# Where tile 5 is transposed, and how the first half of chunk 0 is blocked, in a layernorm, local attention and GLU kernel

## The chip, the cores and the metric

The kernel runs on one core of one Trainium2 chip. The core has five engines that this text names: TensorE (PE in the profile, PEld for its weight loads), VectorE (DVE), ScalarE (ACT), GpSimd (POOL) and SyncE (SP), which issues all of this kernel's DMAs. The metric is the device time of one execution in microseconds (us). The kernel before takes 228.16 us, the median of three runs (227.9 to 228.41).

## What is computed

One layernorm of x (2048 tokens of 512) feeds two branches, whose product is added to x: a dilated local attention (32 heads of 16, 8 positions 2 apart) and a gated linear unit with 1792 inner columns. All inputs and the output are bfloat16.

```python
def reference(A_x, A_wqkv, A_wo, B_x, B_w_gate, B_w_up, B_w_down):
    x = A_x                                        # 1 x 2048 x 512
    xn = layernorm(x)
    # attention: H = 32, Dh = 16, W = 8, dil = 2
    q, k, v = heads(xn @ A_wqkv)
    idx = pos[:, None] - arange(W) * dil           # masked where idx < 0
    logits = einsum("bhsd,bhswd->bhsw", q, k[idx]) * Dh ** -0.5
    s = einsum("bhsw,bhswd->bhsd", softmax(logits), v[idx]) @ A_wo
    # gated linear unit
    h = gelu(xn @ B_w_gate) * (xn @ B_w_up)
    return x + s * silu(h @ B_w_down)
```

## The kernel before

The 2048 tokens are 16 tiles of 128, in four chunks of four tiles (512 tokens). Chunk 0 has the tiles 0 to 3, chunk 1 the tiles 4 to 7. For each chunk j TensorE needs xnT[j], the normalized tokens transposed, so that the 512 features lie on the partitions in four blocks dk.

Order of the program (written out by hand; nothing reorders it, and `at` and `run` only hang pieces of work onto a place in the loops):

- *Loads*, all issued by SP in order: tiles 0 and 1 of x, three row blocks of wqkv, tiles 2 and 3, the last block of wqkv, tiles 4 to 7, then halves of the gate and up weights with the rest of x. A DMA waits for the DMA eight before it, since there are eight completion semaphores that go round.
- *Chunk 0, first half of the tokens (tiles 0 and 1, 256 tokens)*. Six groups of PSUM, `pairs`, hold two output blocks of 128 columns of wqkv each (v in two PSUM tiles of the pool mm, q and k in the tile quad), zeroed first by a matmul with `zero` (L542). `block(dk, ns, i0, n)` (L547 to L557) adds contraction block dk of wqkv to the groups ns for n tokens from i0. Contraction block 0 runs apart for tile 0 (128 tokens) and for tile 1. A tile's way to xnT is: VectorE's statistics (L188, L191), ScalarE's square root (L192), VectorE's reciprocal and `normalize` (xn, L213), four transposes on TensorE into PSUM (L221), and a copy into xnT on ScalarE (L232) or VectorE (L234). Tiles 0 and 1 go in two steps, feature block 0 first and then the other three, through the PSUM tiles tra and trb. The transposes of tiles 2 and 3 stand among the matmuls of block 3 (L593 to L597).
- *Chunk 0, second half (tiles 2 and 3)*. Six groups of two output blocks (L605 to L612); the first group runs in slices of 128 tokens, so that its first half needs tile 2 only. `copy_out` brings q and k to SBUF and v to vst, and SP stores vst to vT in DRAM (L292).
- *GLU of chunk 0*, 14 steps of eight matmuls (g_ps, u_ps; L263). Tiles 4 and 5 are transposed on TensorE ahead of steps 0 and 1. Onto step 0 are also hung, in SP's order: two DMA transposes of tile 6 (`transpose_by_dma`, L255, one DMA for each feature block), the four loads of v from vT with a shift for each position (`load_v`, L308, into v_arr), six DMA transposes (rest of tile 6, tile 7), and the late weights wd and wo (L117, L120). VectorE makes the products of q and k (pk, L334) and h (L449); from step 11 on it makes the products of attention weights and v (pv, L406, eight in all).
- *Chunk 1's projection* (L298, 48 matmuls of 512 tokens, reading all four tiles of xnT[1]), then the down projection of chunk 0 (y_ps, L457, reading wd and h), the denominators and sums (den_ps L372, o_ps L420, reading the eight pv), the logits of chunk 1 (L_ps L352, reading chunk 1's pk), and the output of chunk 0. The other chunks follow in the same way, all their tiles transposed by DMA.

Of the kernel before, what the change touches and what calls it, by code (L numbers as in the profile page):

```python
# [10 lines left out]
BF16 = mybir.dt.bfloat16  # L11
F32 = mybir.dt.float32

P = 128
# [14 lines left out]
def kernel(  # L29
# [13 lines left out]
    nc = tc.nc  # L43
    B, S, D = A_x.shape
    DF = B_w_gate.shape[1]
    NT, NC, NF, NJ = S // P, D // P, DF // P, S // TQ
    TPQ = TQ // P
# [5 lines left out]
    def pool(name, bufs, **kw):  # L53
        return ctx.enter_context(tc.tile_pool(name=name, bufs=bufs, **kw))
# [19 lines left out]
    mm = pool("mm", 4, space=bass.MemoryType.PSUM)  # L74
# [4 lines left out]
    wqkv_sb = wts.tile([P, NC, 3 * D], BF16, name="wqkv_sb")  # L79
# [7 lines left out]
    def load_x(t, n=1):  # L87
        nc.sync.dma_start(
            out=x_sb[:, t : t + n, :],
            in_=x2d[t * P : (t + n) * P, :].rearrange("(t p) d -> p t d", p=P),  # L90
        )
# [7 lines left out]
    def load_wqkv(k):  # L99
        nc.sync.dma_start(out=wqkv_sb[:, k, :], in_=A_wqkv[k * P : (k + 1) * P, :])  # L100

    load_x(0)
    load_x(1)
    load_wqkv(0)
    load_wqkv(1)
    load_wqkv(2)
    load_x(2)
    load_x(3)
    load_wqkv(3)
    load_x(TPQ, TPQ)  # L110
    for i, (lo, hi) in enumerate(((0, DF // 2), (DF // 2, DF))):
        load_w(wg_sb, B_w_gate, lo, hi)
# [19 lines left out]
    ident = const.tile([P, P], BF16, name="ident")  # L132
# [38 lines left out]
    xnT = {}  # L171
# [15 lines left out]
    def first_stats(t):  # L187
        nc.vector.bn_stats(out=stats[:, t, :], in_=x_sb[:, t, :])  # L188

    def first_moments(t):  # L190
        nc.vector.bn_aggr(out=mv[:, t, :], in_=stats[:, t, :])  # L191
        nc.scalar.activation(  # L192
            out=std[:, t, :], in_=mv[:, t, 1:2], func=AF.Sqrt, bias=epsc[:], scale=1.0
        )

    def first_rstd(t):
        nc.vector.reciprocal(out=rstd[:, t, :], in_=std[:, t, :])
# [9 lines left out]
    xns = {}  # L207

    def normalize(t, cs=range(NC)):
        if 0 in cs:  # L210
            xns[t] = xnp.tile([P, D], BF16, name="xn")
        cols = slice(cs[0] * P, (cs[-1] + 1) * P)
        nc.vector.tensor_scalar(  # L213
            out=xns[t][:, cols], in0=x_sb[:, t, cols],
            scalar1=mv[:, t, 0:1], scalar2=rstd[:, t, :],
            op0=ALU.subtract, op1=ALU.mult,
        )

    def to_psum(t, cs, tr):
        for n, c in enumerate(cs):  # L220
            nc.tensor.transpose(  # L221
                tr[:, n * P : (n + 1) * P], xns[t][:, c * P : (c + 1) * P], ident[:]
            )

    def from_psum(t, cs, tr, copy=None):
        j, i = divmod(t, TPQ)
        if j not in xnT:
            xnT[j] = xtp.tile([P, NC, TQ], BF16, name="xnT")
        dst = xnT[j][:, cs[0] : cs[-1] + 1, i * P : (i + 1) * P]
        src = tr.rearrange("p (c n) -> p c n", c=len(cs))  # L230
        if copy is None:
            nc.scalar.activation(out=dst, in_=src, func=AF.Copy)  # L232
        else:
            copy(out=dst, in_=src)  # L234

    def transpose(t, copy=None):
        tr = mm.tile([P, NC * P], BF16, name="tr", tag="mm")
        to_psum(t, range(NC), tr[:])
        from_psum(t, range(NC), tr[:], copy)

    def warm_up(n, cols):

        ps = mm.tile([P, TQ], F32, name="warm_ps", tag="mm")
        for _ in range(n):
            nc.tensor.matmul(  # L245
                ps[:, 0:cols], lhsT=nc.const_aps.tensor(1.0, [P, P], BF16),
                rhs=nc.const_aps.tensor(1.0, [P, cols], BF16), start=True, stop=True,
            )
# [12 lines left out]
    def project(ps, w, lo, j, i0=0, n=TQ):  # L261
        for dk in range(NC):
            nc.tensor.matmul(  # L263
                ps,
                lhsT=w[:, dk, lo : lo + P],
                rhs=xnT[j][:, dk, i0 : i0 + n],
                start=(dk == 0),
                stop=(dk == NC - 1),
            )
# [3 lines left out]
    def copy_out(j, fo, ps, i0=0, n=TQ, m=1, copy=None):  # L273

        which, c = divmod(fo, NC)
        if which == 0:
            if "q" not in st[j]:
                st[j]["q"] = qp.tile([P, NC, TQ], BF16, name="q_sb")
            dst = st[j]["q"][:, c : c + m, i0 : i0 + n]
        elif which == 1:  # L280
            dst = k_sb[j][:, c : c + m, PAD + i0 : PAD + i0 + n]
        else:
            if c // 2 not in st[j]["vst"]:
                st[j]["vst"][c // 2] = vsp.tile([P, 2, TQ], BF16, name="vst")
            dst = st[j]["vst"][c // 2][:, c % 2 : c % 2 + m, i0 : i0 + n]
        if copy is None:
            nc.scalar.activation(out=dst, in_=ps, func=AF.Copy)  # L287
        else:
            copy(out=dst, in_=ps)
        if which == 2 and (c + m) % 2 == 0 and i0 + n == TQ:  # L290
            r, lo = slice((c // 2) * 2 * P, (c // 2 + 1) * 2 * P), PAD + j * TQ
            nc.sync.dma_start(  # L292
                out=vT[r, lo : lo + TQ].rearrange("(c p) n -> p c n", p=P),
                in_=st[j]["vst"][c // 2][:],
            )
# [193 lines left out]
    def at(key, fn, *args):  # L489
        side.setdefault(key, []).append((fn, args))  # L490
# [4 lines left out]

    for i in range(TPQ):
        at(("down", 0, 1), moments, 2 * TPQ + i)
        if i < 2:
            at(("glu", 0, i), transpose, TPQ + i)
        at(("down", 0, 2), normalize, 2 * TPQ + i)  # L500
        at(("glu", 1, 0) if i else ("down", 0, 3), transpose_by_dma, 2 * TPQ + i)
        at(("glu", 1, 10 + i), moments, 3 * TPQ + i)
        at(("qkv", 2, i), normalize, 3 * TPQ + i)
        at(("glu", 2, 0) if i else ("down", 1, 3), transpose_by_dma, 3 * TPQ + i)
# [31 lines left out]
    HQ = TPQ // 2 * P  # L536
    warm_up(6, TQ // 2)
    quad = att.tile([P, NC, 2, HQ], F32, name="qk_ps", tag="quad")
    pairs = [(8 + 2 * i, mm.tile([P, 2, HQ], F32, name="v_ps", tag="mm")[:]) for i in range(2)]
    pairs += [(2 * i, quad[:, i]) for i in range(4)]  # L540
    for _, ps in pairs:
        nc.tensor.matmul(  # L542
            ps, lhsT=zero[:], rhs=nc.const_aps.tensor(1.0, [P, 2, HQ], BF16),
            start=True, stop=False,
        )
    warm_up(4, P)
    def block(dk, ns, i0=0, n=HQ):  # L547
        for b in ns:
            fo, ps = pairs[b]
            for i in range(2):  # L550
                nc.tensor.matmul(  # L551
                    ps[:, i, i0 : i0 + n],
                    lhsT=wqkv_sb[:, dk, (fo + i) * P : (fo + i + 1) * P],
                    rhs=xnT[0][:, dk, i0 : i0 + n],
                    start=False,
                    stop=(dk == NC - 1 and i == 1),
                )  # L557


    one, rest = [0], range(1, NC)  # L560
    tra = mm.tile([P, 2, P], BF16, name="tra", tag="mm")
    trb = mm.tile([P, 2, (NC - 1) * P], BF16, name="trb", tag="mm")
    first_stats(0)
    first_moments(0)
    first_stats(1)
    first_rstd(0)
    first_moments(1)
    normalize(0, one)
    to_psum(0, one, tra[:, 0])
    from_psum(0, one, tra[:, 0])  # L570
    normalize(0, rest)
    to_psum(0, rest, trb[:, 0])
    from_psum(0, rest, trb[:, 0])
    first_rstd(1)
    normalize(1, one)
    normalize(1, rest)
    block(0, range(2), 0, P)
    to_psum(1, one, tra[:, 1])
    from_psum(1, one, tra[:, 1], nc.vector.tensor_copy)
    block(0, range(2, 6), 0, P)  # L580
    to_psum(1, rest, trb[:, 1])
    from_psum(1, rest, trb[:, 1], nc.vector.tensor_copy)
    block(0, range(6), P, P)
    for t in (2, 3):
        first_stats(t)
        first_moments(t)
    nc.scalar.preload_act_table(AF.Gelu_apprx_tanh)
    for t in (2, 3):
        first_rstd(t)
        normalize(t)  # L590
    block(1, range(6))
    block(2, range(6))
    block(3, range(3))  # L593
    transpose(2, nc.vector.tensor_copy)
    block(3, range(3, 5))
    transpose(3, nc.vector.tensor_copy)
    block(3, range(5, 6))  # L597
    for fo, ps in pairs:
        copy_out(0, fo, ps, 0, HQ, 2, nc.vector.tensor_copy if fo >= 8 else None)
    for t in range(TPQ, 2 * TPQ, 2):  # L600
# [3 lines left out]
    sum_constants()  # L604
    for n, fo in enumerate((0, 2, 4, 6, 8, 10)):  # L605
        ps = mm.tile([P, 2, HQ], F32, name="qkv_ps", tag="mm")

        w = HQ if n else P
        for i0 in range(0, HQ, w):
            for i in range(2):  # L610
                project(ps[:, i, i0 : i0 + w], wqkv_sb, (fo + i) * P, 0, HQ + i0, w)
        copy_out(0, fo, ps[:], HQ, HQ, 2)  # L612
    at(("glu", 0, 0), transpose_by_dma, TPQ + 2, (0, 1))
    at(("glu", 0, 0), load_v, 0)
    at(("glu", 0, 0), transpose_by_dma, TPQ + 2, (2, 3))
    at(("glu", 0, 0), transpose_by_dma, TPQ + 3)
    at(("glu", 0, 0), load_late_weights)
    for j in range(NJ):
# [57 lines left out]
```

## Time and profile before

| | |
|---|---|
| median of three runs | 228.16 us |
| profiled execution | 228.41 us, of it 226.7 us span |
| PE busy | 222.4 us (98% of the span), 1342 matmuls |
| DVE busy | 152.2 us (67%) |
| ACT busy | 132.3 us (58%) |
| TensorE clock granted | full in all 40 slices of the span |

The span is what the profiler shows of the engines; the 1.7 us beside it lie around them. "Busy" is an average over stages with different limits, so a stage's own timeline decides what a change in it is worth. The busy shares in 40 slices of 5.67 us (tenths; GB/s is what the DMA engines moved) show how the stages differ: the transfers are full in the first four slices, pause in the fifth, and are busy again up to the eighth:

```profile
PE   8999999999999999999999999999999999999993
...
DVE  5588961999995489969803859925934448971434
...
DMA  6999399942049911100219941100218940001011
GB/s 191 361 397 385 102 211 162 309 121 95 6 99 198 196 48 30 21 1 0 93 34 205 191 112 23 26 6 0 92 25 167 198 113 0 0 3 30 1 39 54
```

In a timeline a row gives start and length in us, engine, line, operation, output and inputs, and in brackets how long the engine stood idle before and what ended that. A row can merge several instructions (x4), and a matmul's row is longer than its share of a stream, because matmuls overlap; the chain in order of time gives each its share of the time.

### The profile page before, as it was taken

How to read it: one execution, taken by the hardware profiler on the slowest of the kernel's cores; microseconds unless marked ns; L12 is line 12 of the kernel's file. 1: busy time of each engine (PE TensorE's matmuls, PEld its weight loads, DVE VectorE, ACT ScalarE, POOL GpSimd, SP SyncE). 2: the span in 40 equal slices, each digit the busy share in tenths (PEclk: the TensorE clock that was granted, in tenths of full speed). 3: DMA queues.
4: the chain of work that ended last, by engine and by line, in shares of the span. 5: the costliest groups of instructions: out<-in, count | busy, mean ns of one | idle time of the engine just before them, and what ended most of it. 6: DMA issues, size and time to landing. Idle time of an engine off the chain costs nothing.

```text
span 226.7 us, 3637 instructions
## 1 busy us (share of the span) xinstructions
PE 222.4 (98%) x1342; PEld 107.9 (48%) x1342; DVE 152.2 (67%) x281; ACT 132.3 (58%) x209; POOL 21.4 (9%) x67
## 2 busy tenths in 40 slices
PE   8999999999999999999999999999999999999993
PEld 4995444444444444444444444444444444444453
DVE  5588961999995489969803859925934448971434
ACT  4388679767631767676752466676763356756210
POOL 1025961000040000320000000000000000000000
PEclk9999999999999999999999999999999999999999
DMA  6999399942049911100219941100218940001011
GB/s 191 361 397 385 102 211 162 309 121 95 6 99 198 196 48 30 21 1 0 93 34 205 191 112 23 26 6 0 92 25 167 198 113 0 0 3 30 1 39 54
DMA packets 30130, 24.64 MB, mean 109 GB/s; under 512 B 10784, under 2 KB 29600, under 8 KB 30112
## 3 DMA queue, kind: packets, MB, share of 16 engines
q1 hardware_dynamic: 30112, 24.41, 45.1%
q8 instruction: 10, 0.16, 0.3%
q14 instruction: 8, 0.07, 0.1%
HBM read 18.74 MB, written 4.34 MB: 102 GB/s over the span
## 4 chain that ended last, share of the span: by engine, by line
PE 98%; DVE 0%; issue 0%; DVEq 0%
PE y_ps L457 21%; PE g_ps L263 21%; PE u_ps L263 21%; PE qkv_ps L263 16%; PE s_ps L473 6%; PE L_ps L352 3%; PE o_ps L420 3%; PE qk_ps L551 2%; PE v_ps L551 1%; PE warm_ps L245 1%; PE qk_ps L542 1%; PE den_ps L372 0%; PE tr L221 0%; PE v_ps L542 0%; PE trb L221 0%; DVE m L481 0%
## 5 line engine op out<-in xcount | busy, mean ns | idle before, releaser
L263 PE MATMUL g_ps<-xnT,wg_sb 128*128 128x512 bf16 x224 | 57.5, 379 | 0.0
L263 PE MATMUL u_ps<-xnT,wu_sb 128*128 128x512 bf16 x224 | 57.5, 379 | 0.0
L457 PE MATMUL y_ps<-wd_sb,h 128*128 128x512 bf16 (+1 forms) x238 | 49.9, 367 | 0.0
L447 ACT ACTIVATE u<-u_ps 128x512 bf16<-128x512 f32 x56 | 33.5, 598 | 16.9 <-PE u_ps L263 16.9
L445 ACT ACTIVATE ge<-g_ps 128x512 bf16<-128x512 f32 x56 | 33.5, 598 | 16.4 <-PE g_ps L263 16.3
L449 DVE TENSOR_TENSOR h<-ge,u 128x512 bf16<-128x512 bf16 x56 | 23.8, 425 | 28.5 <-ACT u L447 26.9
L334 DVE TENSOR_TENSOR pk<-q_sb,k_sb 128x1024 bf16<-128x1024 bf16 (+1 forms) x56 | 39.0, 760 | 4.6 <-ACT k_sb L287 4.6
L406 DVE TENSOR_TENSOR pv<-E,v_arr 128x1024 bf16<-128x1024 bf16 (+1 forms) x48 | 39.7, 862 | 0.3 <-DMA v_arr<-vT 0.3
L263 PE MATMUL qkv_ps<-xnT,wqkv_sb 128*128 128x512 bf16 (+2 forms) x200 | 37.0, 345 | 0.0
L457 PEld LDWEIGHTS <-h 128*128 128x128 bf16 x238 | 23.0, 98 | 25.9 <-issue 1.3
L263 PEld LDWEIGHTS <-wu_sb 128*128 128x128 bf16 x224 | 21.9, 98 | 26.4
L263 PEld LDWEIGHTS <-wg_sb 128*128 128x128 bf16 x224 | 21.7, 98 | 26.3 <-issue 0.8
L465 ACT ACTIVATE sl<-y_ps 128x512 bf16<-128x512 f32 (+1 forms) x17 | 9.7, 572 | 32.6 <-PE y_ps L457 32.6
L263 PEld LDWEIGHTS <-wqkv_sb 128*128 128x128 bf16 x200 | 18.9, 98 | 17.5
L481 DVE TENSOR_TENSOR m<-s_ps,sl 128x512 bf16<-128x512 f32 (+1 forms) x17 | 11.1, 655 | 18.9 <-PE s_ps L473 18.9
L432 DVE TENSOR_TENSOR oT<-o_ps,rb 128x1024 bf16<-128x1024 f32 x8 | 9.4, 1218 | 11.9 <-DMA rb<-rs_d 11.9
L205 POOL TENSOR_TENSOR rstd<-rstd,mhalf 128x1 f32<-128x1 f32 x12 | 8.1, 671 | 71.5 <-DVE rstd L202 71.5
L473 PE MATMUL s_ps<-wo_sb,oT 128*128 128x512 bf16 (+1 forms) x68 | 14.8, 366 | 0.0
L287 ACT ACTIVATE vst<-qkv_ps 128x512 bf16<-128x512 f32 x14 | 8.4, 597 | 3.7 <-PE qkv_ps L263 3.7
L287 ACT ACTIVATE k_sb<-qkv_ps 128x512 bf16<-128x512 f32 x14 | 8.4, 601 | 3.2 <-PE qkv_ps L263 3.2
L473 PEld LDWEIGHTS <-oT 128*128 128x128 bf16 x68 | 6.7, 98 | 7.2
L287 ACT ACTIVATE q_sb<-qkv_ps 128x512 bf16<-128x512 f32 x14 | 8.3, 603 | 3.0 <-PE qkv_ps L263 3.0
(64 smaller groups left out, 130.7 us busy)
## 6 DMA issues: line engine op xcount, KB each, us to landing
v_arr<-vT SPq DMA_DIRECT2D x16, 520.0 KB, 8.6
vT<-vst SPq DMA_DIRECT2D x8, 256.0 KB, 2.2
out_dram<-o_t SPq DMA_DIRECT2D x15, 128.0 KB, 3.2
wg_sb<-in_B_w_gate_dram SPq DMA_DIRECT2D x2, 896.0 KB, 10.0
wu_sb<-in_B_w_up_dram SPq DMA_DIRECT2D x2, 896.0 KB, 11.6
wd_sb<-in_B_w_down_dram SPq DMA_DIRECT2D x1, 1792.0 KB, 9.4
wqkv_sb<-in_A_wqkv_dram SPq DMA_DIRECT2D x4, 384.0 KB, 4.8
x_sb<-in_A_x_dram SPq DMA_DIRECT2D x3, 512.0 KB, 11.3
```

Source lines behind the costliest of these rows:

```text
L263: nc.tensor.matmul(ps, lhsT=w[:, dk, lo : lo + P], rhs=xnT[j][:, dk, i0 : i0 + n], start=(dk == 0), stop=(dk == NC - 1),)
L287: nc.scalar.activation(out=dst, in_=ps, func=AF.Copy)
L334: nc.vector.tensor_tensor(out=st[j]["pk"][w][:, c0 : c0 + n, :], in0=st[j]["q"][:, c0 : c0 + n, :], in1=k_sb[j][:, c0 : c0 + n, off : off ...
L406: nc.vector.tensor_tensor(out=pv[:, d : d + n, :], in0=st[j]["E"][:, wh, :].unsqueeze(1).to_broadcast([P, n, TQ]), in1=st[j]["va"][:, 4 * ...
L432: nc.vector.tensor_tensor(out=oT[:, g : g + 2, :], in0=st[j]["o"][:, g : g + 2, :], in1=st[j]["rb"][:].unsqueeze(1).to_broadcast([P, 2, TQ ...
L445: nc.scalar.activation(out=ge[:], in_=g_ps[:], func=AF.Gelu_apprx_tanh)
L447: nc.scalar.activation(out=u[:], in_=u_ps[:], func=AF.Copy)
L449: nc.vector.tensor_tensor(out=h[:], in0=ge[:], in1=u[:], op=ALU.mult)
L457: nc.tensor.matmul(y[:], lhsT=st[j][fc][:, tt * P : (tt + 1) * P], rhs=wd_sb[:, fc, cols], start=(fc == 0), stop=(fc == NF - 1),)
L465: nc.scalar.activation(out=sl[:], in_=y[:], func=AF.Silu)
L473: nc.tensor.matmul(s[:], lhsT=st[j]["oT"][:, g, tt * P : (tt + 1) * P], rhs=wo_sb[:, g, cols], start=(g == 0), stop=(g == NC - 1),)
L481: nc.vector.tensor_tensor(out=m[:], in0=s[:], in1=sl[:], op=ALU.mult)
```

## The change

The diff does four things.

1. In chunk 0's first half all contraction blocks run over 256 tokens in one loop, block 0 too. Tile 0 is normalized in one operation and transposed into one PSUM tile, from which feature block 0 and then the others are copied; two matmuls of `warm_up` follow. Tile 1 is normalized, transposed and copied in two steps as before, now from one PSUM tile.
2. Tile 2 is transposed at the end of block 2 (before: after three groups of block 3), tile 3 after three groups of block 3 (before: after five).
3. The first group of chunk 0's second half runs over 256 tokens at once, not in slices of 128.
4. Tile 4 is still transposed on TensorE ahead of step 0 of the GLU. Tile 5 is transposed by four DMAs on SP. In SP's queue now five transposes (tile 5, and feature block 0 of tile 6) stand ahead of the four loads of v, and seven (the rest of tile 6, tile 7) behind them; before it was two and six.

The loads at the start are written as loops, in the same order. The helper functions `to_psum` and `from_psum` take the PSUM tile from a table by tile number.

```diff
     def to_psum(t, cs=range(NC)):
+        if 0 in cs:
+            trs[t] = mm.tile([P, NC * P], BF16, name="tr", tag="mm")
+        for c in cs:
             nc.tensor.transpose(
+                trs[t][:, c * P : (c + 1) * P], xns[t][:, c * P : (c + 1) * P], ident[:]
+            )
...
     for i in range(TPQ):
         at(("down", 0, 1), moments, 2 * TPQ + i)
-        if i < 2:
-            at(("glu", 0, i), transpose, TPQ + i)
...
-    normalize(0, one)
-    to_psum(0, one, tra[:, 0])
-    from_psum(0, one, tra[:, 0])
-    normalize(0, rest)
-    to_psum(0, rest, trb[:, 0])
-    from_psum(0, rest, trb[:, 0])
+    normalize(0)
+    to_psum(0)
+    from_psum(0, [0])
+    from_psum(0, rest)
+    warm_up(2, P)
     first_rstd(1)
-    normalize(1, one)
+    normalize(1, [0])
     normalize(1, rest)
-    block(0, range(2), 0, P)
-    to_psum(1, one, tra[:, 1])
-    from_psum(1, one, tra[:, 1], nc.vector.tensor_copy)
-    block(0, range(2, 6), 0, P)
-    to_psum(1, rest, trb[:, 1])
-    from_psum(1, rest, trb[:, 1], nc.vector.tensor_copy)
-    block(0, range(6), P, P)
+    to_psum(1, [0])
+    from_psum(1, [0], nc.vector.tensor_copy)
+    to_psum(1, rest)
+    from_psum(1, rest, nc.vector.tensor_copy)
...
-    block(1, range(6))
-    block(2, range(6))
-    block(3, range(3))
-    transpose(2, nc.vector.tensor_copy)
-    block(3, range(3, 5))
-    transpose(3, nc.vector.tensor_copy)
-    block(3, range(5, 6))
+    for dk in range(NC):
+        for n, (fo, ps) in enumerate(pairs):
+            for i in range(2):
+                nc.tensor.matmul(
+                    ps[:, i, :],
+                    lhsT=wqkv_sb[:, dk, (fo + i) * P : (fo + i + 1) * P],
+                    rhs=xnT[0][:, dk, 0:HQ],
...
+            if (dk, n) in ((2, 5), (3, 2)):
+                transpose(dk, copy=nc.vector.tensor_copy)
...
-        w = HQ if n else P
-        for i0 in range(0, HQ, w):
-            for i in range(2):
-                project(ps[:, i, i0 : i0 + w], wqkv_sb, (fo + i) * P, 0, HQ + i0, w)
+        for i in range(2):
+            project(ps[:, i, :], wqkv_sb, (fo + i) * P, 0, HQ, HQ)
         copy_out(0, fo, ps[:], HQ, HQ, 2)
-    at(("glu", 0, 0), transpose_by_dma, TPQ + 2, (0, 1))
+    at(("glu", 0, 0), transpose, TPQ)
+    at(("glu", 0, 0), transpose_by_dma, TPQ + 1)
+    at(("glu", 0, 0), transpose_by_dma, TPQ + 2, (0,))
     at(("glu", 0, 0), load_v, 0)
-    at(("glu", 0, 0), transpose_by_dma, TPQ + 2, (2, 3))
+    at(("glu", 0, 0), transpose_by_dma, TPQ + 2, (1, 2, 3))
     at(("glu", 0, 0), transpose_by_dma, TPQ + 3)
     at(("glu", 0, 0), load_late_weights)
```

More of the change, by code (lines that the diff above doesn't have):

```diff
@@ L100, in load_wqkv @@
         nc.sync.dma_start(out=wqkv_sb[:, k, :], in_=A_wqkv[k * P : (k + 1) * P, :])
[L102 to L109, printed above, removed]
+    for t in (0, 1):
+        load_x(t)
+    for k in range(NC - 1):
+        load_wqkv(k)
+    for t in (2, 3):
+        load_x(t)
+    load_wqkv(NC - 1)
     load_x(TPQ, TPQ)
@@ L217, in normalize, with to_psum, from_psum @@
         )
-    def to_psum(t, cs, tr):
-        for n, c in enumerate(cs):
+    trs = {}
+    def to_psum(t, cs=range(NC)):
+        if 0 in cs:
+            trs[t] = mm.tile([P, NC * P], BF16, name="tr", tag="mm")
+        for c in cs:
             nc.tensor.transpose(
-                tr[:, n * P : (n + 1) * P], xns[t][:, c * P : (c + 1) * P], ident[:]
+                trs[t][:, c * P : (c + 1) * P], xns[t][:, c * P : (c + 1) * P], ident[:]
             )
-    def from_psum(t, cs, tr, copy=None):
+    def from_psum(t, cs=range(NC), copy=None):
         j, i = divmod(t, TPQ)
@@ L228, in from_psum @@
             xnT[j] = xtp.tile([P, NC, TQ], BF16, name="xnT")
-        dst = xnT[j][:, cs[0] : cs[-1] + 1, i * P : (i + 1) * P]
-        src = tr.rearrange("p (c n) -> p c n", c=len(cs))
+        c = slice(cs[0], cs[-1] + 1)
+        dst = xnT[j][:, c, i * P : (i + 1) * P]
+        src = trs[t][:].rearrange("p (c n) -> p c n", c=NC)[:, c]
         if copy is None:
@@ L236, in transpose @@
     def transpose(t, copy=None):
-        tr = mm.tile([P, NC * P], BF16, name="tr", tag="mm")
-        to_psum(t, range(NC), tr[:])
-        from_psum(t, range(NC), tr[:], copy)
+        to_psum(t)
+        from_psum(t, copy=copy)
     def warm_up(n, cols):
@@ L546 @@
     warm_up(4, P)
-    def block(dk, ns, i0=0, n=HQ):
-        for b in ns:
-            fo, ps = pairs[b]
-            for i in range(2):
[L551 to L562, printed above, removed]
+    rest = range(1, NC)
     first_stats(0)
@@ L590 @@
         normalize(t)
-    block(1, range(6))
-    block(2, range(6))
-    block(3, range(3))
-    transpose(2, nc.vector.tensor_copy)
-    block(3, range(3, 5))
-    transpose(3, nc.vector.tensor_copy)
-    block(3, range(5, 6))
+    for dk in range(NC):
[5 more added lines that the diff above has]
+                    rhs=xnT[0][:, dk, 0:HQ],
+                    start=False,
+                    stop=(dk == NC - 1 and i == 1),
+                )
+            if (dk, n) in ((2, 5), (3, 2)):
+                transpose(dk, copy=nc.vector.tensor_copy)
     for fo, ps in pairs:
@@ L606 @@
         ps = mm.tile([P, 2, HQ], F32, name="qkv_ps", tag="mm")
-        w = HQ if n else P
-        for i0 in range(0, HQ, w):
-            for i in range(2):
-                project(ps[:, i, i0 : i0 + w], wqkv_sb, (fo + i) * P, 0, HQ + i0, w)
+        for i in range(2):
+            project(ps[:, i, :], wqkv_sb, (fo + i) * P, 0, HQ, HQ)
         copy_out(0, fo, ps[:], HQ, HQ, 2)
-    at(("glu", 0, 0), transpose_by_dma, TPQ + 2, (0, 1))
+    at(("glu", 0, 0), transpose, TPQ)
+    at(("glu", 0, 0), transpose_by_dma, TPQ + 1)
+    at(("glu", 0, 0), transpose_by_dma, TPQ + 2, (0,))
     at(("glu", 0, 0), load_v, 0)
-    at(("glu", 0, 0), transpose_by_dma, TPQ + 2, (2, 3))
+    at(("glu", 0, 0), transpose_by_dma, TPQ + 2, (1, 2, 3))
     at(("glu", 0, 0), transpose_by_dma, TPQ + 3)
```

## The prediction

> **What bounds the kernel.** I read the page's chain of waits first, then the chain in order of time, then the timelines of SP, VectorE and TensorE up to 62 us, because every line the diff touches runs before that.
>
> ```profile
> PE 98%; DVE 0%; issue 0%; DVEq 0%
> ```
> ```profile
> 59.24 1.80 PE L_ps L352 x32
> ```
>
> The first line is the page's shares of the chain by engine, the second a piece of it in order of time (start, us). TensorE is the chain nearly throughout: a microsecond put into its queue or a wait in front of it is a microsecond of time. The one piece to keep in mind is the second chunk's logits, L_ps at 59.24: 1.80 us here, 1.73 in chunks 2 and 3. The missing 0.07 is a wait for VectorE (its timeline: start, us, idle time before in brackets):
>
> ```profile
> 39.83 0.43 DVE L449 TENSOR_TENSOR h<-ge,u 128x512 bf16<-128x512 bf16 x1 [0.56 <-ACT u L447]
> 40.59 1.22 DVE L406 TENSOR_TENSOR pv<-E,v_arr 128x2048 bf16<-128x2048 bf16 x1 [0.34 <-DMA v_arr<-vT]
> ...
> 45.01 5.76 DVE L406 TENSOR_TENSOR pv<-E,v_arr 128x2048 bf16<-128x2048 bf16 x5
> 50.68 9.71 DVE L334 TENSOR_TENSOR pk<-q_sb,k_sb 128x1024 bf16<-128x1024 bf16 x16
> 60.32 0.95 DVE L385 RECIPROCAL rs<-den_ps 128x128 bf16<-128x128 f32 x1
> ```
>
> From 40.59 VectorE has no gap up to the last pk at 50.68 + 9.71 = 60.39. L_ps takes its 32 matmuls 0.054 us apart from record 59.07; the 28th, due at 60.53, needs that last pk. So in chunk 0 TensorE and VectorE arrive together, and VectorE's stretch begins with a wait for v. A later landing of v goes through 19.8 us of VectorE work to TensorE, with no slack. What v waits for is in SP's queue:
>
> ```profile
> 17.12 2.87 SPq L292 DMA_DIRECT2D vT<-vst  x2
> 20.09 2.71 SPq L255 DMA_TRANSPOSE xnT<-xn  x2
> 25.85 2.70 SPq L308 DMA_DIRECT2D v_arr<-vT  x4
> 28.59 8.87 SPq L255 DMA_TRANSPOSE xnT<-xn  x6
> 38.29 0.40 SPq L117 DMA_DIRECT2D wd_sb<-in_B_w_down_dram  x1
> ```
>
> SP stands idle from 22.80 (second transpose, 21.57 + 1.23) to 25.85, when the second store of v lands (issued 18.12, to landing 7.7). The four loads of v then take 5.6, 7.6, 11.0 and 12.6 us from their issues: the last, issued 27.90, lands at 40.5.
>
> **The change, part by part.**
>
> *Start, on TensorE.* The gate is tile 2 of x:
>
> ```profile
> 8.41 0.69 DVE L188 BATCH_NORM_STATS2 stats<-x_sb 128x6 f32<-128x512 bf16 x1 [0.94 <-DMA x_sb<-in_A_x_dram]
> ...
> 10.20 0.41 DVE L213 TENSOR_SCALAR xn<-x_sb,mv,rstd 128x512 bf16<-128x512 bf16 x1
> ```
> ```profile
> 10.59 0.38 PE L551 MATMUL qk_ps<-xnT,wqkv_sb 128*128 128x256 bf16 x2
> 10.80 0.39 PE L221 MATMUL tr<-ident,xn 128*128 128x128 bf16 x4
> ...
> 11.69 0.38 PE L551 MATMUL qk_ps<-xnT,wqkv_sb 128*128 128x256 bf16 x2
> 11.90 1.28 PE L263 MATMUL qkv_ps<-xnT,wqkv_sb 128*128 128x128 bf16 x18
> ```
>
> xn of tile 2 is done at 10.61 and its transposes start at 10.80; the load and VectorE's order there stay as they are.
>
> 1. Block 0 begins later. One xn of 512 columns (0.41) replaces 128 (0.28), so tile 0's transposes start about 5.15, not 5.06. Tile 1 is now one PSUM tile, whose last three transposes wait by the program for the copy of the first. From the rows: xn's first columns done 5.19 + 0.31 = 5.50, transpose 5.73, done 6.02, copy 6.13 to 6.35, next transposes about 6.48, three at 0.055, block 0 at 6.65. Its 12 matmuls of 256 columns (8 take 0.87 in the chain, 0.109 each) end at 7.95; before, 24 of 128 columns (8 take 0.45) ended at 7.53. The two new warm-up matmuls (0.06 to 0.11 each) lie in the wait before 5.73. Cost so far +0.42.
> 2. Blocks 1 and 2 (24 x 0.109 = 2.62) end at 10.57. The transposes of tile 2 now come next and must wait for 10.80, so what step 1 cost is swallowed by that wait, up to 0.23 more. But before, six matmuls of block 3 were done by 10.80; now all twelve are behind: 6 x 0.109 = +0.65.
> 3. Tile 3's transposes then start at 11.02 + 0.65 = 11.67, and its copy (0.42) ends about 12.52, just where block 3 ends (12.55). The first pair projected in 256 columns needs it at once. A wait of 0 to 0.1; I take 0.03, since the numbers nearly meet. Its 16 matmuls of 128 become 8 of 256: 0.90 - 0.87 = -0.03.
> 4. Tile 5 leaves TensorE: four transposes, 0.22 in the chain at 19.29. Its ScalarE copy (0.59) goes too; TensorE waited for neither there.
>
> TensorE alone: 0.65 + 0.03 - 0.03 - 0.22 = +0.43 (0.35 to 0.8: block 0 late by 0.2 beyond its cover, the copy's 0.1).
>
> *SP's queue.* Four transposes are added: three more ahead of the loads of v, one more behind. The third starts at 22.85. Starts lie 1.25 to 1.38 apart where nothing holds them (28.59, 29.97, 31.30, 32.55), 1.28 in chunk 1. Three at 1.28 bring the first load of v to 26.7 in place of 25.85: 3.05 us of wait cover 3.05 of 3.9. In addition TensorE's +0.65 delays the copies to vst and so the stores of v. The second store took 1.88 us to issue against 0.89 for the first: about 1.0 of it is a queue held by the weights still moving (about 400 GB/s until 22), which stays where it is and absorbs most of the slip. Bounds 0 and 0.62; I take 0.15, nearest to the absorbed end. The store's landing (25.8, at most 26.4) no longer decides. First load of v at 26.9: +1.05.
>
> *How long v then takes.* Before: 14.65 from the first issue (25.85) to the last landing. The program lets a DMA wait for the one eight before it; six transposes still go before the third load has landed, the seventh waits for that landing, in the place of wd's load. So I take 14.65 again. With four transposes behind them the loads of chunk 1 took 13.75 (64.67 to 78.4), with none in chunk 3 13.3: per transpose 0.1 to 0.45, so bounds -0.2 and +0.45. v lands at 41.55.
>
> *What queues behind.* The transposes landed 0.4 to 1.8 us after v before (40.9 to 42.3). The seventh lands near 43.9; the projection needs its last block at 43.74 + 0.43 + 0.65 = 44.8. Covered by 0.9, and TensorE has 0.6 to spare before L_ps. wd is issued at about 41.6 instead of 38.29 and, with its 9.4 us, lands by 51; y_ps reads it from 54.1. Covered by 3.
>
> [...] Four transposes at 19.29 cost TensorE 0.22, and one on SP 1.20 to 1.43. [...] In a stream the trace has 0.055 each.
>
> *Sum.* The two delays run side by side and the later sets the end: TensorE +0.43, v +1.05. TensorE then stalls about 0.6 in the L_ps of chunk 1. Nothing behind it is tied to a fixed time, so it is not won back. The profiled execution took 228.41 (span 226.7, 1.7 around it): 229.46. It lies 0.25 above the median, so on the median 228.16 + 1.05 = **229.2**.
>
> **Rivals.**
>
> - *TensorE alone sets the end* (v hardly late): transposes at 1.20 apart (the shortest row), no slip, v 0.2 quicker: 3.6 - 3.05 - 0.2 = +0.35, below 0.43. Time 228.6. Against: SP's starts are never closer than 1.25 where transposes follow each other.
> - *One added transpose is held.* The one at 32.55 took 2.36, 1.13 above the others, behind four loads of v:
>
> ```profile
> 32.55 2.36 SPq L255 DMA_TRANSPOSE xnT<-xn  x1
> ```
>
>  The fourth and fifth transposes stand behind less (x and the stores land by 25.8), but if one is held as there: 1.05 + 1.13 = +2.2, time 230.3.
> - *Not slower: the first loads drain 0.65 us or more sooner.* Both costs hang on that backlog: x tile 2 lands at 8.4, and SP's second store is held until 20. If x tile 2 came by 7.75, the wait at 10.80 would be gone and TensorE's sum be 0.43 - 0.65 = -0.22; SP's hold of 1.0 would fall, the first transpose start at 19.1 and v be issued at 25.7, -0.15. Time 228.0. Against: order and sizes of the loads are unchanged until the stores of v, and the three runs before differ by 0.5 in all.
>
> **How the numbers follow.** Forecast 0.62 (its own range 228.8 to 229.9), TensorE alone 0.14, a held transpose 0.15, the earlier drain 0.06, something else 0.03. The range 228.5 to 230.3 takes in the forecast, most of the first rival and about half of the second. About 0.2% (0.46 us) is what a measurement of this kernel can tell from no change. Half of "TensorE alone" and the drain fall within it: same 0.13; faster 0.03; slower 0.84.
>
> **What will show it.** Five transposes on SP from about 20.1 and the first load of v near 26.9; the pv behind a wait for v of about 1 us, starting near 41.6; an L_ps of chunk 1 of 2.4 us in the chain in place of 1.80; tile 2's transposes still at 10.80, the projection about 12.55. Wrong if pv starts before 41, if L_ps stays at 1.8, or if TensorE waits at the projection of chunk 1 or at y_ps for wd.

## The result, and the profile after

| | median us | runs | ratio to before, 95% interval |
|---|---|---|---|
| before | 228.11 | 6 (227.9 to 228.41) | |
| changed | 229.16 | 6 (228.67 to 229.88) | 1.0047 (1.0028 to 1.0066) |

The changed kernel is slower by 1.05 us, between 0.6 and 1.5. The forecast was 229.2. Its runs spread over 1.2 us, those of before over 0.5, and the profiled execution, 228.67 with a span of 227.0, is the fastest of the six, while that of before, 228.41, is the slowest of its six. A second profile of the changed kernel, at 229.21 with a span of 227.5, lies at the median; both are used below.

The page's chain of waits of the changed kernel, shares by engine and then by line, no longer names TensorE alone:

```profile
PE 80%; DVE 10%; DMA 6%; SPq 1%; issue 1%; ACT 0%; DVEq 0%; ACTq 0%
PE y_ps L460 20%; PE g_ps L266 18%; PE u_ps L266 18%; PE qkv_ps L266 11%; PE s_ps L476 6%; DMA v_arr<-vT 5%; DVE pk L337 4%; DVE pv L409 3%; PE o_ps L423 2%; PE L_ps L355 2%; PE qk_ps L576 2%; DMA x_sb<-in_A_x_dram 1%; SPq L311 1%; PE v_ps L576 1%; DVE h L452 1%
```

The order in time shows the way: SP issues the loads of v, the loads move, VectorE makes pv and pk, and TensorE goes on with L_ps. First SP's timeline:

```profile
17.16 2.52 SPq L295 DMA_DIRECT2D vT<-vst  x2
19.77 6.73 SPq L258 DMA_TRANSPOSE xnT<-xn  x5
26.61 2.71 SPq L311 DMA_DIRECT2D v_arr<-vT  x4
29.37 10.10 SPq L258 DMA_TRANSPOSE xnT<-xn  x7
```

There is no idle time left between the transposes and the loads of v. The first load goes out at 26.61 where it was 25.85. VectorE's timeline, from the first pv to the last pk:

```profile
40.98 1.23 DVE L409 TENSOR_TENSOR pv<-E,v_arr 128x2048 bf16<-128x2048 bf16 x1 [0.91 <-DMA v_arr<-vT]
...
45.40 5.76 DVE L409 TENSOR_TENSOR pv<-E,v_arr 128x2048 bf16<-128x2048 bf16 x5
51.08 9.71 DVE L337 TENSOR_TENSOR pk<-q_sb,k_sb 128x1024 bf16<-128x1024 bf16 x16
```

The wait for v has grown from 0.34 to 0.91, and the last pk ends at 60.79. TensorE's timeline breaks at the 28th of the 32 matmuls of L_ps, the one that reads that pk:

```profile
58.88 1.74 PE L355 MATMUL L_ps<-pk,dsum 128*32 128x512 bf16 x27
60.84 0.59 PE L355 MATMUL L_ps<-pk,dsum 128*32 128x512 bf16 x5 [0.23 <-DVE pk L337]
61.37 0.82 PE L460 MATMUL y_ps<-wd_sb,h 128*128 128x512 bf16 x3
```

At an even 0.054 apart the 28th would have come at 58.88 + 27 x 0.054 = 60.34; it came 0.50 later. The starts are not even, though (most fourth ones come 0.206 after the one before), so the whole stretch tells more. From the first L_ps to the y_ps behind it the kernel before takes 1.91:

```profile
59.07 1.98 PE L352 MATMUL L_ps<-pk,dsum 128*32 128x512 bf16 x32
60.98 0.82 PE L457 MATMUL y_ps<-wd_sb,h 128*128 128x512 bf16 x3
```

The changed kernel takes 2.49 (58.88 to 61.37), 0.58 more. From the y_ps at 61.37 to the end of the span it is 165.6 us. Before it is 165.7 (60.98 to 226.7), and in every profile of this study it is 165.6 or 165.7. All that the change and the experiments do is done by then.

### The profile page after: what moved, and what is told of

It is laid out like the page before. It is cut to its first block, busy times and chain, and to the rows that moved or that the text cites. A ratio compares the mean times of both kernels' runs of the same rounds, so it can differ in the third digit from the quotient of the medians.

```text
span 227.0 us, 3597 instructions
## 1 busy us (share of the span) xinstructions
PE 222.2 (98%) x1320; PEld 106.9 (47%) x1320; DVE 152.1 (67%) x280; ACT 131.7 (58%) x208; POOL 19.9 (9%) x67
## 4 chain that ended last, share of the span: by engine, by line
PE 80%; DVE 10%; DMA 6%; SPq 1%; issue 1%; ACT 0%; DVEq 0%; ACTq 0%
PE y_ps L460 20%; PE g_ps L266 18%; PE u_ps L266 18%; PE qkv_ps L266 11%; PE s_ps L476 6%; DMA v_arr<-vT 5%; DVE pk L337 4%; DVE pv L409 3%; PE o_ps L423 2%; PE L_ps L355 2%; PE qk_ps L576 2%; DMA x_sb<-in_A_x_dram 1%; SPq L311 1%; PE v_ps L576 1%; DVE h L452 1%
## 5 line engine op out<-in xcount | busy, mean ns | idle before, releaser
L266 PE MATMUL qkv_ps<-xnT,wqkv_sb 128*128 128x512 bf16 (+1 forms) x192 | 37.0, 352 | 0.0
L484 DVE TENSOR_TENSOR m<-s_ps,sl 128x512 bf16<-128x512 f32 (+1 forms) x17 | 11.1, 655 | 18.5 <-PE s_ps L476 18.5
```

What stands on the lines that cost most here:

```text
L266: nc.tensor.matmul(ps, lhsT=w[:, dk, lo : lo + P], rhs=xnT[j][:, dk, i0 : i0 + n], start=(dk == 0), stop=(dk == NC - 1),)
L484: nc.vector.tensor_tensor(out=m[:], in0=s[:], in1=sl[:], op=ALU.mult)
```

## The experiments

Times in us. Profile times below are of one execution each; the medians are of 4 to 12 executions, each compared with runs of the kernel before on the same chip.

| kernel | median us | ratio to before, 95% interval |
|---|---|---|
| old_start_new_queue | 228.77 | 1.0028 (1.0014 to 1.0041) |
| new_start_old_queue | 228.65 | 1.0020 (1.0011 to 1.0029) |
| two_products_less | 228.47 | 1.0010 (0.9996 to 1.0025) |
| eight_ahead | 232.93 | 1.0211 (1.0194 to 1.0228) |
| four_ahead | 228.49 | 1.0015 (1.0003 to 1.0027) |
| old_start_four_ahead | 227.93 | 0.9989 (0.9980 to 0.9998) |
| whole_block_0_only | 228.48 | 1.0015 (1.0006 to 1.0024) |
| tile_1_in_two | 228.73 | 1.0018 (1.0009 to 1.0027) |
| two_ahead | 228.15 | 1.0004 (0.9995 to 1.0013) |

**Each half of the change alone.** old_start_new_queue is the kernel before with only the queue of the change:

```diff
-        if i < 2:
-            at(("glu", 0, i), transpose, TPQ + i)
...
-    at(("glu", 0, 0), transpose_by_dma, TPQ + 2, (0, 1))
+    at(("glu", 0, 0), transpose, TPQ)
+    at(("glu", 0, 0), transpose_by_dma, TPQ + 1)
+    at(("glu", 0, 0), transpose_by_dma, TPQ + 2, (0,))
     at(("glu", 0, 0), load_v, 0)
-    at(("glu", 0, 0), transpose_by_dma, TPQ + 2, (2, 3))
+    at(("glu", 0, 0), transpose_by_dma, TPQ + 2, (1, 2, 3))
```

> The start of the kernel before (blocks split by tile), with tile 5 by DMA and five transposes ahead of the loads of v. If the landing of v sets the end through VectorE, the first load of v is issued near 26.7 and the time stays about 0.8 to 1.1 us above the kernel before: 228.9 to 229.2. If TensorE's start is what was paid, the time is that of before less the four transposes of tile 5: 227.9.

228.77: v costs 0.6 here, with the old start and with tile 5's transposes off TensorE. That is below the 0.8 to 1.1 expected, and clear of 227.9. Its TensorE has the same break:

```profile
58.54 1.94 PE L352 MATMUL L_ps<-pk,dsum 128*32 128x512 bf16 x27
60.70 0.59 PE L352 MATMUL L_ps<-pk,dsum 128*32 128x512 bf16 x5 [0.23 <-DVE pk L334]
```

new_start_old_queue is the changed kernel with the queue lines of before and tile 5 back on TensorE ahead of step 1.

> The changed start, with tile 5 on TensorE and two transposes ahead of the loads of v, six behind, as before. If the landing of v sets the end, only the start is left: the first load of v at 25.9, L_ps of chunk 1 about 1.8 us, and the time 0 to 0.65 above before, 228.1 to 228.8, by how early tile 2 of x lands. If the start is what was paid, the time is that of the changed kernel plus tile 5's 0.2: 229.2 to 229.4.

228.65, within the band of "only the start is left". VectorE begins pv with a gap too short to be named, and L_ps runs through:

```profile
40.48 1.23 DVE L409 TENSOR_TENSOR pv<-E,v_arr 128x2048 bf16<-128x2048 bf16 x1
```
```profile
59.16 1.95 PE L355 MATMUL L_ps<-pk,dsum 128*32 128x512 bf16 x32
```

So each half costs something: the start 0.46, the queue 0.58, both 1.05.

**Is it VectorE's stretch?** two_products_less is the changed kernel without chunk 1's last product of q and k:

```diff
         for w in ws:
+            if j == 1 and w == W - 1:
+                st[j]["pk"][w] = st[j]["pk"][w - 1]
+                continue
```

> The changed kernel without chunk 1's last product of q and k (two pk operations, 1.2 us of VectorE; the logits read the product of position 6 in its place, so the attention of that position is left out). If VectorE's stretch from the landing of v to the last pk sets the end, L_ps of chunk 1 no longer waits and the time falls by 0.5 to 1.1 us to 228.0 to 228.6. If the delay sits in TensorE's own queue, it stays at 229.2.

228.47, 0.69 below the changed kernel. In the profiled execution v came later than in any profile of the changed kernel, and still cost TensorE nothing. VectorE's timeline, then TensorE's:

```profile
42.15 1.22 DVE L412 TENSOR_TENSOR pv<-E,v_arr 128x2048 bf16<-128x2048 bf16 x1 [1.65 <-DMA v_arr<-vT]
...
52.24 8.51 DVE L340 TENSOR_TENSOR pk<-q_sb,k_sb 128x1024 bf16<-128x1024 bf16 x14
```
```profile
59.44 1.98 PE L358 MATMUL L_ps<-pk,dsum 128*32 128x512 bf16 x32
```

Since only VectorE's work was taken away, this shows that VectorE's stretch was the bound. What remains, 228.47 - 228.19 = 0.28 (-0.1 to 0.6), is left for TensorE's own sum.

**How it goes with the number ahead.** eight_ahead puts all four transposes of tile 6 ahead of the loads of v (the first added line), four_ahead puts all four behind (the second):

```diff
-    at(("glu", 0, 0), transpose_by_dma, TPQ + 2, (0,))
+    at(("glu", 0, 0), transpose_by_dma, TPQ + 2)      # eight_ahead
     at(("glu", 0, 0), load_v, 0)
-    at(("glu", 0, 0), transpose_by_dma, TPQ + 2, (1, 2, 3))
+    at(("glu", 0, 0), transpose_by_dma, TPQ + 2)      # four_ahead
```

> The changed kernel with eight transposes ahead of the loads of v and four behind. If v's issue sets the end one for one, three more starts of 1.28 put the first load of v near 30.5, and the time is 3.8 us above the changed kernel, about 233.0, less what four transposes behind in place of seven save (0.1 to 0.45 each): 231.8 to 233.0. If v has cover somewhere, it is less than 1 us above the changed kernel.

232.93, 3.77 above the changed kernel for three more starts (3 x 1.28 = 3.8). SP's timeline, then VectorE's:

```profile
19.71 11.62 SPq L258 DMA_TRANSPOSE xnT<-xn  x8
31.38 3.35 SPq L311 DMA_DIRECT2D v_arr<-vT  x4
```
```profile
45.28 1.23 DVE L409 TENSOR_TENSOR pv<-E,v_arr 128x2048 bf16<-128x2048 bf16 x1 [4.73 <-DMA v_arr<-vT]
```

The medians say that past the point where SP's wait is used up, a transpose ahead of v costs its whole start. In the profile the sum has more terms: the first load of v went out 4.55 later than in the mean of the changed kernel's two profiles, since one of the eight transposes took 2.46, and from there to the first pv it took 13.90 where they have 14.37 and 14.45. TensorE also waited, for the last transposes, at the projection of chunk 1:

```profile
46.27 1.45 PE L266 MATMUL qkv_ps<-xnT,wqkv_sb 128*128 128x512 bf16 x6 [2.06 <-DMA xnT<-xn]
```

That wait costs nothing here, since v is later still: L_ps then waits for VectorE another 2.2.

> The changed kernel with four transposes ahead of the loads of v and eight behind. The four end near 25.4, inside SP's wait for the stores of v, so if v's issue sets the end the first load goes out at 25.4 to 25.9 as before and the time is TensorE's own: 0 to 0.65 above before, 228.1 to 228.8. The eighth transpose behind waits for the last load of v and lands near 43; if that is too late, TensorE waits at the projection of chunk 1 instead. If the start is what was paid, 229.2.

228.49, within the band, and the same as two_products_less: with v in time the changed kernel pays its start alone. The profiled execution (228.79) is not a clean one. One of its four transposes took 2.46, so its loads went out at 26.67, not 25.4:

```profile
23.99 2.46 SPq L258 DMA_TRANSPOSE xnT<-xn  x1
```

old_start_four_ahead is old_start_new_queue with the same edit as four_ahead.

> The start of the kernel before with tile 5 by DMA, four transposes ahead of the loads of v and eight behind. If v is in time and the start costs nothing, the four transposes that left TensorE are won only if VectorE's stretch allows it: 227.9 to 228.1, no worse than before. If the eighth transpose behind is late, TensorE waits at the projection of chunk 1 and the time is above 228.3.

227.93: below both kernels, by 0.02 to 0.2% against before, 0.23 us in the medians. Its four transposes took 5.28, the first load of v went out at 25.40 when the stores had landed, and pv did not wait for v. This is the version that the experiments point to.

two_ahead, shown against the kernel before, keeps its start and moves all the additional transposes behind the loads:

```diff
-        if i < 2:
-            at(("glu", 0, i), transpose, TPQ + i)
...
-    at(("glu", 0, 0), transpose_by_dma, TPQ + 2, (0, 1))
+    at(("glu", 0, 0), transpose, TPQ)
+    at(("glu", 0, 0), transpose_by_dma, TPQ + 1, (0, 1))
     at(("glu", 0, 0), load_v, 0)
-    at(("glu", 0, 0), transpose_by_dma, TPQ + 2, (2, 3))
+    at(("glu", 0, 0), transpose_by_dma, TPQ + 1, (2, 3))
+    at(("glu", 0, 0), transpose_by_dma, TPQ + 2)
```

> The start of before with tile 5 by DMA, two transposes ahead of the loads of v and ten behind. v is in time (first load at 25.1 to 25.9). By the waits of the program the ninth to twelfth transposes go out only as the loads of v and the transposes before them land, the last near 43, and land near 44.5, about 0.4 to 1.0 after the projection of chunk 1 wants them. VectorE's stretch hides part of that. Time 227.9 to 228.8, and if above 228.2 with TensorE waiting at the projection of chunk 1, L263, for xnT.

228.15, no difference from before. The late landing is there, though small: in its profile (228.03) the last transpose goes out at 41.86 and lands at 44.19, and the projection's fourth matmul, the first to read that block, starts at 44.23, 0.49 behind the third where they otherwise follow at 0.216. The projection takes 10.64 (43.30 to 53.94), against 10.36 in old_start_four_ahead, whose last transpose lands at 42.42. These 0.28 are about what the median lies above that kernel's, 0.22.

**What in the start costs.** whole_block_0_only is the changed kernel with block 0 alone left of the change; the rest of the start, tile 5 and the queue are those of before:

```diff
-            if (dk, n) in ((2, 5), (3, 2)):
-                transpose(dk, copy=nc.vector.tensor_copy)
+            if (dk, n) in ((3, 2), (3, 4)):
+                transpose(n // 2 + 1, copy=nc.vector.tensor_copy)
...
-        for i in range(2):
-            project(ps[:, i, :], wqkv_sb, (fo + i) * P, 0, HQ, HQ)
+        w = HQ if n else P
+        for i0 in range(0, HQ, w):
+            for i in range(2):
+                project(ps[:, i, i0 : i0 + w], wqkv_sb, (fo + i) * P, 0, HQ + i0, w)
```

> The kernel before with block 0 alone changed (256 tokens at once, tile 0 and tile 1 each in one PSUM tile): tiles 2 and 3 are transposed where they were, the first group is sliced, the queue is that of before. If the wait for tile 2 of x at 10.80 is what the changed start costs (the prediction's step 2, 0.65 from the place of the transposes), this costs only block 0's later begin, at most 0.42, and less than new_start_old_queue. If TensorE comes to tile 2 by its own work, block 0's begin is all, and the time equals new_start_old_queue's 228.65.

228.48. That is 0.28 above the kernel before on its chip (228.20) and below 228.65, as the first expectation has it, but the interval overlaps that of new_start_old_queue: by the time alone inconclusive. tile_1_in_two gives tile 1's last three transposes a PSUM tile of their own:

```diff
-        if 0 in cs:
+        if 0 in cs or t == 1:
             trs[t] = mm.tile([P, NC * P], BF16, name="tr", tag="mm")
```

> new_start_old_queue with tile 1's transposes in two PSUM tiles, so that its last three do not wait for the copy of the first. If block 0's begin sets the start, it comes 0.2 to 0.4 earlier than 6.7 and the time falls from 228.65 to 228.3 to 228.5. If the wait for tile 2 of x sets it, the time stays at 228.65.

228.73, no gain, but the edit didn't do what it was for: in the new tile the transposes wait for ScalarE's copies of tile 0 (0.21, in place of 0.32 for VectorE's copy), and block 0 begins at 6.60 where after_again has 6.70. It says nothing on the theories.

The profiles decide where the times don't. Below is TensorE's start in the second profile of the changed kernel, and then in the first:

```profile
5.08 0.61 PE L224 MATMUL tr<-ident,xn 128*128 128x128 bf16 x4
...
6.54 0.33 PE L224 MATMUL tr<-ident,xn 128*128 128x128 bf16 x3 [0.32 <-DVE xnT L238]
6.70 0.60 PE L576 MATMUL v_ps<-xnT,wqkv_sb 128*128 128x256 bf16 x4
...
10.73 0.40 PE L224 MATMUL tr<-ident,xn 128*128 128x128 bf16 x4
```
```profile
4.92 0.40 PE L224 MATMUL tr<-ident,xn 128*128 128x128 bf16 x4
...
6.04 0.33 PE L224 MATMUL tr<-ident,xn 128*128 128x128 bf16 x3 [0.32 <-DVE xnT L238]
6.21 0.60 PE L576 MATMUL v_ps<-xnT,wqkv_sb 128*128 128x256 bf16 x4
```

From block 0's begin to tile 2's transposes it is 6.70 to 10.73, 4.03, of which 36 x 0.109 = 3.92 is matmuls. TensorE comes to tile 2 by its own work and waits 0.1 there. What sets the start is when block 0 begins, and that differs by 0.5 between the two. Two other profiles agree: from block 0's begin to the projection of chunk 1 it is 37.52 (6.30 to 43.82) in whole_block_0_only and 37.51 (6.32 to 43.83) in new_start_old_queue, so the new places of tiles 2 and 3 cost nothing that shows.

**Two profiles more.**

> The kernel before once more, for a second profile. If the landing of tile 2 of x varies from run to run, its statistics start at another time than 8.41, and the transposes of tile 2 with it.

The statistics of tile 2 began at 7.87 there, 0.54 earlier. Over the profiles of this study they begin between 7.76 and 8.50, whichever kernel it is. In this second profile (228.12) pv did not wait for v at all:

```profile
39.59 0.43 DVE L449 TENSOR_TENSOR h<-ge,u 128x512 bf16<-128x512 bf16 x1 [0.56 <-ACT u L447]
39.94 1.22 DVE L406 TENSOR_TENSOR pv<-E,v_arr 128x2048 bf16<-128x2048 bf16 x1
```

The last load was issued at 27.16 and took 12.0, so v landed at 39.2, about 0.7 before the pv.

> The changed kernel once more, for a second profile. If v's landing explains the time, a run at 229.0 to 229.5 has v's wait end at 41.3 to 41.8 and an L_ps of chunk 1 that ends as much later as the run is longer than 228.67.

229.21: pv began at 41.50 after 0.89 of waiting for v, and L_ps ended so that y_ps began at 61.89, 0.52 later than in the first profile, for 0.54 more time.

## Why the prediction was right, step by step

- *v sets the end through VectorE and shows as a break in L_ps*: as put, and shown by taking VectorE's work away. The stall was forecast at 0.6; from the first L_ps to the y_ps behind it, it is 2.49 and 2.47 in the two profiles, 0.58 and 0.56 above the 1.91 of before. Two of the signs that were named did not hold in the first profile: its pv began at 40.98, just under the 41 that was to mean "wrong", and tile 2's transposes began at 10.19, not 10.80. In the second they are 41.50 and 10.73.
- *The two delays run side by side and the later sets the end*: with TensorE's 0.28 (two_products_less) against v's 1.05 this holds. That the halves alone, 0.46 (0.24 without tile 5's 0.22 on TensorE) and 0.58, nearly add up seems to contradict it, but they meet earlier: the new start delays the stores of v. The second store goes out at 18.12 and 17.77 in the two profiles of before and at 18.04 and 18.58 in those of the changed kernel, the first load of v at 25.85 and 25.12 against 26.61 and 27.05, and at 26.47 in old_start_new_queue. new_start_old_queue shows it with the queue of before: its first load goes out at 26.10.
- *How the two delays meet*: where v is in time, VectorE's stretch moves with TensorE: in new_start_old_queue, old_start_four_ahead and before_again the last pk ends 16.63 after the projection of chunk 1 begins. Where v is late, the stretch begins with v and takes 19.81 from the first pv to the last pk. In the changed kernel the last pk is then 0.60 and 0.58 later than 16.63, in old_start_new_queue 0.81, in four_ahead's profile 0.28 and in eight_ahead 2.20; L_ps to y_ps is longer than the 1.88 of before_again by nearly the same, 0.61, 0.59, 0.81, 0.28 and 2.20.
- *v issued 1.05 later*: 1.35 in the mean of two profiles each; 0.76 in the two that were profiled first. The terms: from the third start to the first load it is 4.06 and 3.89 (3 x 1.28 = 3.84 forecast). The first transpose starts at 20.09 and 19.36 in the profiles of before and at 19.77 and 20.37 in those of the changed kernel, a slip of 0.34 in the mean, where I took 0.15 with bounds of 0 and 0.62.
- *14.65 us from the first issue to the last landing*: mis-sized. From the first issue to the first pv it is 14.37 and 14.45 in the changed kernel; in the profile of before it was 14.74. That one had a slow landing: its last load took 12.6, and 11.9 to 12.4 in the eleven other profiles with six to ten transposes behind (11.1 in eight_ahead, with four). A seventh transpose behind cost nothing that shows.
- *No slack*: wrong as stated. That one execution waited 0.34 for v; in the second v landed 0.7 ahead of the pv, and VectorE's stretch had another 0.39 of gaps (20.20 from the first pv to the last pk, where 19.81 is enough). The larger delay of the issue, the shorter landing and this slack offset each other, and the time came out as forecast partly for that reason.
- *TensorE +0.43*: 0.28 measured, below my bounds of 0.35 to 0.8, though its interval (-0.1 to 0.6) reaches into them. Its step 2 fell: it let tile 2's transposes wait 0.23 for tile 2 of x, until 10.80, and there is hardly a wait. The rows of before did not show that gate: the two matmuls ahead of those transposes start at 10.59 and take 0.109 each, so TensorE was busy until 10.80. Step 1's begin of block 0, 6.65 forecast, is 6.70 in one profile and 6.21 in the other; the wait of tile 1's transposes for the copy, which step 1 read from the program, is there with 0.32. The copy of tile 3 (step 3) costs nothing.
- *The rivals*: "one added transpose is held" happens in some executions (2.46 in four_ahead and eight_ahead, 2.03 in two_products_less, none of those ahead of v above 1.46 in the two profiles of the changed kernel) and would fit its spread up to 229.88. In all three the held transpose ends 0.16 before the second store of v lands (26.24 against 26.40 in eight_ahead, 26.41 against 26.57 in two_products_less, 26.45 against 26.61 in four_ahead), but no run moved that landing alone; what holds it stays open. "TensorE alone" is what is left when v is in time: 228.47 and 228.49, against 228.6 forecast. That transposes never start closer than 1.25 apart, the reason given against it, is not so (78.87 and 80.01 in the profile of before), but in the changed kernel's profiles the five ahead of v start 1.26 to 1.52 apart. The earlier drain of the loads nearly occurred (tile 2 of x at 7.93, 0.48 earlier where the rival asked for 0.65), and the time did not come to 228.0: TensorE was hardly waiting for that tile. The late landings behind v, which I had covered by 0.9 and 3 us, cost nothing in the changed kernel; with ten transposes behind (two_ahead) the last one did cost about 0.28.

## What to carry to other kernels

An idle stretch in an issuing queue can serve as a budget, to be measured: here SP's 3.05 us ahead of the loads of v paid for two more transposes of 1.28 us (old_start_four_ahead, first load at 25.40) and not for three (26.61 and 27.05 in the changed kernel), and three more past it (eight_ahead) cost 3.77 at an engine three steps away, where three starts of 1.28 are 3.84. Before an engine's stretch is called free of slack, its wait should be seen in more than one execution: in one profile of the kernel before VectorE waited 0.34 for v, and in the other v landed about 0.7 ahead of the pv. And when two halves of a change are measured apart, ask where their delays meet before they are added.

## What was not expected of the hardware

The same matmuls near the start take up to twice the time in one execution that they take in another: the four transposes of tile 0 take 0.22 in the chain in new_start_old_queue and 0.43 in after_again (0.055 and 0.108 each), and the two warm-up matmuls behind them 0.13 and 0.23. Later in after_again the four transposes of tile 2 are back at 0.23 (10.73 to 10.96). The clock that the profile calls granted does not show it: it is 1.00 in each microsecond from 2 to 8 in both. What sets the pace, and when it changes, was not shown. Ahead of block 0 the changed start has ten matmuls of 128 columns from tile 0's transposes on (after_again, from 5.08), the kernel before four (from 5.06), and in the profiles of the new start block 0 begins at 6.2 to 6.3 where tile 0's transposes take the shorter time and at 6.6 to 6.8 where they take the longer one. The runs of tile_1_in_two fall in two groups, 228.43 to 228.48 and 228.71 to 228.78. The profiled one, 228.74, has the longer time (5.06 to 5.48 for the four); that the groups are the two paces is likely, not shown.
